# Eight small products and two low parts at other places in one core's adaLN block

## The chip, the cores and the metric

The kernel runs on one core of one Trainium2 chip. The metric is the device time of one execution in microseconds (us). The five engines work through queues of their own and wait for each other by semaphores: TensorE (PE) multiplies matrices into PSUM, VectorE (DVE), ScalarE (ACT) and GpSimd (POOL) do elementwise work, and SyncE (SP) issues most of the transfers.

## The reference

A layer norm with a scale and a shift from a conditioning vector feeds a linear-attention block, and its result is added to x; a second layer norm of the same kind feeds a bilinear GLU without a nonlinearity, which is added again:

```
h = _layernorm(x) * (1 + ca) + sa
x = x + ga * _A_ref(h, A_wqkv, A_wo)          # 2048 x 512, 32 heads of 16
h = _layernorm(x) * (1 + cb) + sb
x = x + gb * _B_ref(h, w_gate, w_up, w_down)  # ((h Wg) * (h Wu)) Wd, F = 1376
```

Everything is float32. This study concerns the second half, from the GLU on.

## The kernel before

Each float32 operand is split into a high part h (rounded by an ACT copy) and a low part l = x - h (a subtraction on DVE or POOL), and each product is three matmuls, h·h, h·l and l·h.

**The blocks.** The 2048 tokens are four chunks of 512, taken in two sides: side 0 is chunks 0 and 1, side 1 chunks 2 and 3. The 1376 columns of the GLU are eleven f tiles, ten of 128 and f tile 10 (`tail`) of 96. The main loop goes over 22 blocks, n = 0 to 21: eleven f tiles of side 0, then eleven of side 1. The text names a block by n: blocks 11 and 12 are the first two of side 1, block 21 is the last (f tile 10 of side 1). A block computes the gate and up products of both chunks with Strassen's seven products (Winograd's form), each of six matmuls of 512 columns, in four PSUM banks a, b, c, d. In order they are: a11 into a, s1 into d, s2 into b, a12 into a, s3 into c, a22 into c, s4 into d. Between them ACT and DVE copy and add banks: c22 = d + u3 (L1113) reads d behind s3; c12 = d + u2 (L1122) reads d behind s4; phi (L1083) are the two elementwise products of gate and up. The s1 of the next block overwrites d.

**The points.** Between the products lie named points, `a11`, `s1`, `s2`, `a12`, `s3`, `pe`, `mid`, `s4`, at each of which a list of small jobs is run, in the list's order. `s3` and `pe` follow each other with no product between them; `mid` lies between a22 and s4; `s4` is the end of the block. The order in which the code runs is the order on every engine's queue.

**The down products.** f tiles are paired, and a pair's product with w_down is again done by seven products, in a form with 256 columns: `pair_steps` returns seven steps (L1226 on PE, with the adds to x, L1253, on DVE). They wait in `queue`, and a block pops one at each of the points s1, s1, a12, a12, pe, pe, s4. The high and low parts of a pair's operands come from `Pair.second` and `Pair.lows` (L1168 on ACT, L1172 on DVE or POOL). f tile 10 has no partner. Its eight products of side 0, one for each chunk and each 128 tokens, are in the list `alone`: a single product is three matmuls of 512 columns with 96 rows (L1146, L1147, L1148), one add to x on DVE (L1153), and the store of x on SP's queue (L1155). Four singles are run in block 11 and four in block 12. All pair steps and singles take a bank from a pool of four PSUM banks, `acc`; a bank is free again when DVE has added it to x.

**Transfers.** The right operands of later blocks (right, seven loads for a block, L1044) and the rows of w_down (raw, L111) are loaded on SP's queue, in the order of the code, behind the stores of x. The raw rows are scaled on DVE (L1280) before they are split.

Of the kernel before, what the change touches and what calls it, by code (L numbers as in the profile page):

```python
# [22 lines left out]
def tile_adaln_block(  # L23
# [24 lines left out]
    NF = len(fts)  # L48
# [1383 lines left out]
    tail = groups[-1][-1]  # L1432
# [8 lines left out]
    for n, (s, g, f) in enumerate(order):  # L1441
# [10 lines left out]
        at = {p: list(early.get((n, p), ())) for p in ("a11", "s1", "s2", "s3", "mid", "s4", "pe")}  # L1452
# [39 lines left out]
        if (s, f) in pair_of:  # L1492
            at_first = f == groups[g][0]
            p = pairs.setdefault((s, g), Pair())
# [20 lines left out]
        if was and was[:2] in paired and was[2] == groups_of[was[0]][was[1]][1]:  # L1515
            of, p = was[0], pairs[was[:2]]
            points = POINTS if queue else POINTS[4:]
            queue += [x for js in ((0, 1), (2, 3))[:1 if (s, f) == (1, tail) else 2] for x in pair_steps(of, p, js)]
            if of:
                at["s2"].append(lambda p=p: (p.lows("s1", "s2"), p.second("s4")))  # L1520
                at.setdefault("a12", []).append(lambda p=p: p.lows("a12", "s4", "a22"))
            else:
                at["s2"].append(lambda p=p: p.second("s1", "s2"))
                at.setdefault("a12", []).append(lambda p=p: p.lows("s1", "s2", "a22", "a12"))
                at["pe"].append(lambda p=p: p.second("s4"))
                at["s4"].append(lambda p=p: p.lows("s4"))
        for x in points if queue else ():
            at.setdefault(x, []).append(lambda: queue and queue.pop(0)())
        points = POINTS
        if s == 1 and alone:  # L1530
            for x in ("s3", "pe", "mid", "s4"):
                at[x].insert(0, lambda: alone.pop(0)())
        if f == tail and s == 1:
            at["s3"].append(lambda: split_down(1, tail))
# [66 lines left out]
```

## Time and profile before

| | us |
|---|---|
| median of 3 runs (lowest, highest) | 556.5 (555.55, 557.04) |
| the profiled execution | 555.82 |
| its span, first to last instruction | 553.4 |
| PE busy in the span | 546.1 |
| DVE busy | 432.5 |
| ACT busy | 299.7 |
| POOL busy | 177.6 |

The profile is of one execution. A row of its timeline has the start from the span's start, the duration, the engine, the line in the kernel, the operation with its output and inputs, and how many such instructions were merged; in brackets stands how long the engine was idle before it, and what ended that. PE rows give the weights' shape and the output's. SPq is SP's sequencer, which issues transfers. The mean granted clock of TensorE over the span is 0.998 of full speed.

### The profile page before, as it was taken

Reading aid. Unit: us, or ns where it says so; the run is one execution under the profiler, and the core shown is the slowest. Engines: PE = TensorE matmul, PEld = TensorE weight load, DVE = VectorE, ACT = ScalarE, POOL = GpSimd, SP = SyncE. Lnnn points to the kernel's source line nnn. Section 1 sums busy time; section 2 is a strip of 40 time slices with the busy share of each in tenths; the row PEclk is TensorE's granted clock in tenths of the full one; section 3 lists DMA queues with packets and bytes.
Section 4 is the critical chain, followed back from the end, with each engine's and each line's share of the span. In section 5 each row is a group of like instructions: output and inputs, shape, how many; then the busy total and the mean of one; then the engine's idle time right before and its main releaser. Section 6 shows DMA issues by size and latency. Waiting matters only on the chain.

```text
span 553.4 us, 8143 instructions
## 1 busy us (share of the span) xinstructions
PE 546.1 (99%) x2775; PEld 460.0 (83%) x2775; DVE 432.5 (78%) x794; ACT 299.7 (54%) x535; POOL 177.6 (32%) x180
## 2 busy tenths in 40 slices
PE   7999999999999999999999999999999999999997
PEld 6888888888888888888888888878888888888886
DVE  5978779978998998865655766896676877779696
ACT  4876858456467876654545355553243535443540
POOL 2000000003527646353556644540003524242400
PEclk9999999999999999999999999999999999999999
DMA  8910224203230045194888634299667534442004
GB/s 248 374 62 1 76 77 152 77 0 78 78 114 2 0 161 181 39 322 173 284 286 279 215 123 172 77 341 390 199 217 259 176 129 139 136 145 78 1 0 153
DMA packets 58512, 83.24 MB, mean 150 GB/s; under 512 B 6564, under 2 KB 23720, under 8 KB 58472
## 3 DMA queue, kind: packets, MB, share of 16 engines
q1 hardware_dynamic: 56544, 81.16, 43.2%
q10 hardware_dynamic: 1928, 1.58, 1.0%
q8 instruction: 22, 0.36, 0.3%
q14 instruction: 18, 0.15, 0.1%
HBM read 53.02 MB, written 29.69 MB: 149 GB/s over the span
## 4 chain that ended last, share of the span: by engine, by line
PE 94%; DVE 3%; DMA 2%; issue 0%; ACT 0%; POOL 0%; DVEq 0%; ACTq 0%; POOLq 0%
PE bank L1057 36%; PE acc L1226 9%; PE acc L871 8%; PE bank L219 5%; PE bank L221 5%; PE bank L220 5%; PE acc L1147 3%; PE acc L1146 3%; PE acc L1148 3%; PE acc L372 3%; PE acc L374 3%; PE acc L373 3%; PE bank L284 2%; PE acc L459 2%; PE bank L846 1%; DMA raw<-in_B_w_down_dram 1%
## 5 line engine op out<-in xcount | busy, mean ns | idle before, releaser
L1057 PE MATMUL bank<-h,w 128*128 128x512 f32 (+1 forms) x924 | 222.2, 391 | 0.2 <-DVE g L1122 0.2
L1057 PEld LDWEIGHTS bank<-h,w 128*128 128x128 f32 (+1 forms) x924 | 168.1, 186 | 36.4 <-DVE g L1122 0.6
L1063 ACT ACTIVATE bank<-bank 128x512 f32<-128x512 f32 (+2 forms) x46 | 26.2, 571 | 123.8 <-PE bank L1057 123.6
L1253 DVE TENSOR_TENSOR x<-acc,x 128x256 f32<-128x256 f32 x132 | 48.0, 415 | 12.9 <-PE acc L1226 12.2
L1226 PE MATMUL acc<-w,kh 128*128 128x256 f32 x308 | 57.4, 283 | 0.4 <-DVE x L1253 0.4
L1226 PEld LDWEIGHTS acc<-w,kh 128*128 128x128 f32 x308 | 50.6, 191 | 4.4 <-DVE x L1253 0.6
L1020 POOL TENSOR_TENSOR w<-raw,w 128x256 fp32r<-128x256 f32 (+3 forms) x22 | 24.7, 1124 | 73.7 <-ACT w L1013 64.1
L219 PE MATMUL bank<-w,h 128*128 128x512 f32 x112 | 44.1, 394 | 0.0
L221 PE MATMUL bank<-w,h 128*128 128x512 f32 x112 | 43.7, 390 | 0.0
L220 PE MATMUL bank<-w,h 128*128 128x512 f32 x112 | 43.7, 390 | 0.0
L1226 PE MATMUL acc<-w,kl 128*128 128x256 f32 x154 | 43.5, 283 | 0.0
L871 PE MATMUL acc<-w,xh 128*128 128x512 f32 x128 | 40.7, 399 | 0.0
L712 POOL TENSOR_TENSOR f<-h,zb 128x512 f32<-128x512 f32 x12 | 17.4, 1470 | 62.9 <-ACT zb L692 48.8
L262 POOL TENSOR_TENSOR rstd<-ve,half 128x4 f32<-128x4 f32 (+3 forms) x12 | 11.2, 936 | 81.6 <-DVE ve L259 68.5
L1063 ACT ACTIVATE u<-bank 128x512 f32<-128x512 f32 (+1 forms) x44 | 26.2, 595 | 15.4 <-PE bank L1057 15.2
L1083 DVE TENSOR_TENSOR phi<-bank,g 128x512 f32<-128x512 f32 (+1 forms) x22 | 15.1, 687 | 24.2 <-PE bank L1057 24.2
L1113 DVE TENSOR_TENSOR g<-bank,u 128x512 f32<-128x512 f32 (+1 forms) x22 | 15.2, 690 | 21.2 <-ACT u L1063 19.9
L1020 POOL TENSOR_TENSOR w<-t,w 128x512 fp32r<-128x512 f32 (+1 forms) x22 | 29.7, 1351 | 0.0
L1153 DVE TENSOR_TENSOR x<-acc,x 128x512 f32<-128x512 f32 x44 | 27.8, 680 | 2.3 <-PE acc L1148 2.3
L1147 PE MATMUL acc<-w,kh 128*128 128x512 f32 (+1 forms) x76 | 29.6, 390 | 0.0
L1146 PE MATMUL acc<-w,kh 128*128 128x512 f32 (+1 forms) x76 | 29.6, 390 | 0.0
L1148 PE MATMUL acc<-w,kl 128*128 128x512 f32 (+1 forms) x76 | 29.6, 389 | 0.0
(204 smaller groups left out, 1184.0 us busy)
## 6 DMA issues: line engine op xcount, KB each, us to landing
right<-w SPq DMA_DIRECT2D x56, 256.0 KB, 3.6
w<-right SPq DMA_DIRECT2D x56, 256.0 KB, 3.7
x<-in_A_x_dram SPq DMA_DIRECT2D x22, 256.0 KB, 5.3
raw<-in_w_mod_dram SPq DMA_DIRECT2D x22, 256.0 KB, 3.7
raw<-in_B_w_down_dram SPq DMA_DIRECT2D x18, 256.0 KB, 2.9
side_s<-h SPq DMA_DIRECT2D x16, 256.0 KB, 2.5
h<-side_s SPq DMA_DIRECT2D x16, 256.0 KB, 5.4
raw<-in_A_wqkv_dram SPq DMA_DIRECT2D x12, 256.0 KB, 5.9
```

Of the source, the lines that this page charges most:

```text
L219: nc.tensor.matmul(ps, ah, bh, start=begin and i == 0, stop=False)
L220: nc.tensor.matmul(ps, ah, bl, start=False, stop=False)
L221: nc.tensor.matmul(ps, al, bh, start=False, stop=end and i == n - 1)
L871: nc.tensor.matmul(yps[i], x, y, start=fresh and k + n == 0, stop=k == KD - 1 and n == 2, skip_group_check=True)
L1020: sub = lambda out, x, y: (on or nc.gpsimd).tensor_tensor(out, x, f32(y), op=ALU.subtract)
L1057: mm = lambda x, y, **kw: nc.tensor.matmul(ps, x[:, k], y, skip_group_check=True, **kw)
L1063: nc.scalar.activation(out, x, AF.Copy)
L1146: nc.tensor.matmul(dn[j], hh[:n, a:b], dh[:n], start=i == 0, stop=False)
L1147: nc.tensor.matmul(dn[j], hh[:n, a:b], dl[:n], start=False, stop=False)
L1148: nc.tensor.matmul(dn[j], hl[:n, a:b], dh[:n], start=False, stop=i == n_of - 1)
L1226: mm = lambda x, y, **kw: nc.tensor.matmul(ps, x[:, a:b], y, skip_group_check=True, **kw)
L1253: nc.vector.tensor_tensor(xt[:, halves[at]], banks[b][m], xt[:, halves[at]], op=ALU.add)
```

## The change

```diff
@@ -1518,7 +1518,8 @@
             if of:
                 at["s2"].append(lambda p=p: (p.lows("s1", "s2"), p.second("s4")))
-                at.setdefault("a12", []).append(lambda p=p: p.lows("a12", "s4", "a22"))
+                if f != tail:
+                    at.setdefault("a12", []).append(lambda p=p: p.lows("a12", "s4", "a22"))
...
@@ -1527,8 +1528,10 @@
         for x in points if queue else ():
             at.setdefault(x, []).append(lambda: queue and queue.pop(0)())
         points = POINTS
+        if (s, f) == (1, tail):
+            at["a12"].append(lambda p=p: p.lows("a12", "s4", "a22"))
         if s == 1 and alone:
-            for x in ("s3", "pe", "mid", "s4"):
+            for x in ("s3", "s3", "pe", "pe") if n == NF else ("s3", "s3", "pe", "pe"):
                 at[x].insert(0, lambda: alone.pop(0)())
```

There are two edits. In blocks 11 and 12 the four singles stood at s3, pe, mid and s4; they now stand two at s3 and two at pe, which is one place on PE, between the products s3 and a22 (both arms of the conditional are the same). In block 21 the low parts of a12, s4 and a22 of the last pair stood ahead of the two pair steps at a12; they now stand behind them.

On PE, block 12: the rows with acc are singles (each three rows), bank_2389 is the product a22 into c, bank_2390 the product s4 into d. This piece of the difference shows the second single's end and the two that move up:

```order
 L1147 MATMUL acc_4526<-w_4317,kh_4289 128x512
 L1148 MATMUL acc_4526<-w_4316,kl_4290 128x512
+L1146 MATMUL acc_4532<-w_4316,kh_4285 128x512
+L1147 MATMUL acc_4532<-w_4317,kh_4285 128x512
+L1148 MATMUL acc_4532<-w_4316,kl_4286 128x512
+L1146 MATMUL acc_4538<-w_4316,kh_4285 128x512
+L1147 MATMUL acc_4538<-w_4317,kh_4285 128x512
+L1148 MATMUL acc_4538<-w_4316,kl_4286 128x512
 L1057 MATMUL bank_2389<-h_4232,w_3849 128x512
 L1057 MATMUL bank_2389<-h_4233,w_3849 128x512
```

The third and fourth single left the places behind a22 and behind s4 and now stand ahead of a22; twelve matmuls of singles follow each other.

On DVE, block 12, before: the adds of the singles are L1153, g_4518 is c22, phi_4551 and phi_4554 the products, g_4550 is c12.

```order
L1113 TENSOR_TENSOR g_4518<-bank_2390,u_4516 128x512
L1153 TENSOR_TENSOR x_99<-acc_4520,x_99 128x512
L1153 TENSOR_TENSOR x_101<-acc_4526,x_101 128x512
L1153 TENSOR_TENSOR x_131<-acc_4538,x_131 128x512
L1083 TENSOR_TENSOR phi_4551<-bank_2389,g_4518 128x512
L1122 TENSOR_TENSOR g_4550<-bank_2390,u_4490 128x512
L1083 TENSOR_TENSOR phi_4554<-g_4492,g_4550 128x512
L1153 TENSOR_TENSOR x_133<-acc_4556,x_133 128x512
```

And the same place now:

```order
L1113 TENSOR_TENSOR g_4518<-bank_2390,u_4516 128x512
L1153 TENSOR_TENSOR x_99<-acc_4520,x_99 128x512
L1153 TENSOR_TENSOR x_101<-acc_4526,x_101 128x512
L1153 TENSOR_TENSOR x_131<-acc_4532,x_131 128x512
L1153 TENSOR_TENSOR x_133<-acc_4538,x_133 128x512
L1083 TENSOR_TENSOR phi_4557<-bank_2389,g_4518 128x512
L1122 TENSOR_TENSOR g_4556<-bank_2390,u_4490 128x512
L1083 TENSOR_TENSOR phi_4560<-g_4492,g_4556 128x512
```

The fourth add moved from behind the block's last phi to the other three. On SP's queue the order is unchanged: four stores of x, seven loads of right, two of w_down.

On DVE, block 21: s_5883 is the sum s4 of the pair, kl are low parts (5845 of a12, 5886 of s4), the rows L1253 the adds of the two pair steps at a12, g_5925 is c22.

```order
 L1182 TENSOR_TENSOR s_5883<-phi_5818,s_5852 128x512
-L1172 TENSOR_TENSOR kl_5845<-phi_5818,kh_5844 128x512
-L1172 TENSOR_TENSOR kl_5886<-s_5883,kh_5885 128x512
 L1253 TENSOR_TENSOR x_1867<-acc_5785,x_1867 128x256
 L1253 TENSOR_TENSOR x_1869<-acc_5785,x_1869 128x256
 L1253 TENSOR_TENSOR x_2045<-acc_5783,x_2045 128x256
 L1253 TENSOR_TENSOR x_2047<-acc_5783,x_2047 128x256
+L1172 TENSOR_TENSOR kl_5845<-phi_5818,kh_5844 128x512
+L1172 TENSOR_TENSOR kl_5886<-s_5883,kh_5885 128x512
 L1113 TENSOR_TENSOR g_5925<-bank_2390,u_5923 96x512
```

The two low parts changed places with the four adds.

## The prediction

> **What bounds the kernel now.** I began with the page: the busy shares, the clock, the chain of waits.
>
> ```profile
> PE 546.1 (99%) x2775; PEld 460.0 (83%) x2775; DVE 432.5 (78%) x794; ACT 299.7 (54%) x535; POOL 177.6 (32%) x180
> PEclk9999999999999999999999999999999999999999
> PE 94%; DVE 3%; DMA 2%; issue 0%; ACT 0%; POOL 0%; DVEq 0%; ACTq 0%; POOLq 0%
> ```
>
> TensorE (PE) is busy almost from end to end at a full clock. The change neither adds nor removes a matmul, so it can only open or close gaps between matmuls. The list of waits on PE, for the whole span, says how much there is to win:
>
> ```profile
> PE acc L153 <- DVE w L148: 2.0, 1, 2.0
> PE bank L295 <- ACT n L277: 1.0, 1, 1.0
> PE acc L1226 <- DVE x L1253: 0.4, 1, 0.4
> PE bank L1057 <- DVE g L1122: 0.2, 1, 0.2
> ```
>
> The first two are in the first 10 us, far from the change. This list counts from the modelled end of a matmul, and modelled ends overlap; a gap is better read from start to start. One of 512 columns starts 0.23 us after its predecessor, one of 256 columns 0.12 us after it, as these pieces of the chain show:
>
> ```profile
> 387.85 1.36 PE bank L1057 x6
> 393.35 1.43 PE acc L1226 x12
> ```
>
> Against these pitches I read the timeline of the stretches that the edits touch. Blocks are counted as in the program's loop: 11 and 12 carry the moved products, 21 is the last. Three gaps stand out. The first is in block 11:
>
> ```profile
> 382.61 0.40 PE L1146 MATMUL acc<-w,kh 96*128 96x512 f32 x1
> 383.44 0.69 DVE L1113 TENSOR_TENSOR g<-bank,u 128x512 f32<-128x512 f32 x1 [1.26 <-ACT u L1063]
> 384.00 0.40 PE L1226 MATMUL acc<-w,kh 128*128 128x256 f32 x2
> 384.05 1.28 DVE L1153 TENSOR_TENSOR x<-acc,x 128x512 f32<-128x512 f32 x2
> 384.60 0.28 PE L1226 MATMUL acc<-w,kl 128*128 128x256 f32 x1
> 384.79 0.51 PE L1226 MATMUL acc<-w,kh 128*128 128x256 f32 x2
> ```
>
> The matmul at 384.79 opens the pair step "d" in a bank that the first single product still holds until VectorE (DVE) has added it to x. That add starts at 384.05 and, being one of two in 1.28 us with 0.68 each, ends at 384.73; PE goes on 0.06 later. It starts 0.19 after its predecessor instead of 0.12, and its pair takes 0.51 instead of 0.40, a restart that costs 0.11. Together 0.18 us.
>
> The second is at the end of block 13:
>
> ```profile
> 402.33 5.27 SPq L1155 DMA_DIRECT2D out_dram<-x  x4
> 407.69 3.25 SPq L1044 DMA_DIRECT2D w<-right  x7
> 411.06 1.05 SPq L111 DMA_DIRECT2D raw<-in_B_w_down_dram  x2
> 414.35 0.74 DVE L1253 TENSOR_TENSOR x<-acc,x 128x256 f32<-128x256 f32 x2
> 416.63 1.29 DVE L1280 TENSOR_TENSOR raw<-raw,row 128x512 f32<-128x512 f32 x2 [1.54 <-DMA raw<-in_B_w_down_dram]
> 417.41 1.55 PE L1057 MATMUL bank<-h,w 128*128 128x512 f32 x6
> 417.84 0.68 DVE L1083 TENSOR_TENSOR phi<-bank,g 128x512 f32<-128x512 f32 x1
> 418.44 0.68 DVE L1122 TENSOR_TENSOR g<-bank,u 128x512 f32<-128x512 f32 x1
> 419.18 1.67 PE L1057 MATMUL bank<-h,w 128*128 128x512 f32 x6 [0.22 <-DVE g L1122]
> ```
>
> DVE stands 1.54 us at the scaling of the w_down rows, which land late; phi and c12 (L1122) queue behind it, and PE needs c12 read before it overwrites bank d. PE was due at 417.41 + 1.36 = 418.77 and starts at 419.18: 0.41, with 1.67 - 1.55 = 0.12 for the restart, 0.5 us in all.
>
> The third is in block 21:
>
> ```profile
> 528.55 0.68 DVE L1182 TENSOR_TENSOR s<-phi,s 128x512 f32<-128x512 f32 x1
> 529.15 0.68 DVE L1172 TENSOR_TENSOR kl<-phi,kh 128x512 fp32r<-128x512 f32 x1
> 530.06 0.69 DVE L1172 TENSOR_TENSOR kl<-s,kh 128x512 fp32r<-128x512 f32 x1 [0.23 <-ACT kh L1168]
> 530.67 1.41 DVE L1253 TENSOR_TENSOR x<-acc,x 128x256 f32<-128x256 f32 x4
> 530.83 0.28 PE L1226 MATMUL acc<-w,kl 128*128 128x256 f32 x1
> 531.47 0.51 PE L1226 MATMUL acc<-w,kh 128*128 128x256 f32 x2 [0.37 <-DVE x L1253]
> 532.00 0.68 DVE L1113 TENSOR_TENSOR g<-bank,u 96x512 f32<-96x512 f32 x1
> 532.30 2.95 PE L1057 MATMUL bank<-h,w 128*96 128x512 f32 x12
> ```
>
> The next "d" step again lacks a bank: the adds that free it (L1253) stand behind two low parts (L1172), the second of which waits for ScalarE. PE is due 0.12 after 530.83, at 530.95, and starts at 531.47: 0.52, and 0.11 for the restart, 0.63 us.
>
> **The change part by part.** Low parts of the last block. DVE's order becomes s, four adds, two low parts. The adds start at 529.15 and take 1.41, and the pair that frees the bank (half of them) is through before 530. PE's "d" at 530.95 no longer waits: -0.63. What is late next? The low parts end at 530.56 + 2 x 0.6 = 531.8 and c22 (L1113) behind them at 532.4, instead of 532.7 before, since it too lay behind the waiting low part. PE overwrites d in the second half of the twelve matmuls from 532.30, half of 2.95 later and now 0.63 earlier, at 533.1: spare 0.7. The low parts themselves are read by pair steps behind those twelve matmuls, past 534. POOL's low part of a22 has no other place in POOL's order. Nothing here costs.
>
> Singles in block 11. All twelve matmuls now run from 382.61 at (384.00 - 382.61) / 6 = 0.232 each, to 385.39; "a" follows, and "d" 0.72 later at 386.11. DVE's four adds start at 384.05 and end at 384.73, 385.33, 385.93 and 386.53 (0.60 from one to the next). Four banks are in turn: "a" takes the first single's (free 384.8, needed 385.4), its ScalarE seed the second's, "d" the third's, free at 385.93 + 0.06 = 385.99, needed at 386.11. The gap closes with 0.12 to spare: -0.18. From both sides: were the third bank a whole add late, the gap would be 0.6 - 0.12 + 0.11 = 0.6; nothing excludes a few hundredths of wait. I take no wait, since every term is a row of this place.
>
> The Trainium skill speaks against this: VectorE: DVE Perf Modes, The DRAIN you can't avoid, says that an operation does not start until the pipe of the one before is empty. By that rule the adds would stand 0.68 apart, the third would end at 386.1, and with the restart 0.15 us of the gap would stay, which would make the sum below 1.16. The two adds of this trace, 1.28 us for both, do not bear it out.
>
> Singles in block 12. This block has no pair steps behind its singles, so what they covered matters more:
>
> ```profile
> 400.19 0.40 PE L1146 MATMUL acc<-w,kh 96*128 96x512 f32 x1
> 401.62 1.28 DVE L1153 TENSOR_TENSOR x<-acc,x 128x512 f32<-128x512 f32 x2
> 403.66 1.53 PE L1057 MATMUL bank<-h,w 128*128 128x512 f32 x6
> 405.22 0.69 DVE L1122 TENSOR_TENSOR g<-bank,u 128x512 f32<-128x512 f32 x1
> 405.72 6.97 PE L1057 MATMUL bank<-h,w 128*128 128x512 f32 x30
> 406.55 0.68 DVE L1153 TENSOR_TENSOR x<-acc,x 128x512 f32<-128x512 f32 x1
> ```
>
> The fourth single used to lie between the last product into d and the next block. That cover goes. Now: singles from 400.19 to 402.97, two products of 1.36 to 405.69, the next block's first 1.36, and d is overwritten at 407.05. The last product into d starts at 404.33; c12 starts 405.22 - 403.66 = 1.56 behind that, at 405.89, and is done at 406.58. Spare 0.4 us, so no cost; were phi or an add in front of it, 0.68 more would cost PE 0.3 and the restart. The adds no longer stand there: they run from 401.62 at 0.60 and are done at 404.1.
>
> Its queue. The four stores of x keep their places on SP's queue, and behind them the seven loads of right parts and the two of w_down. The last store waited for the add that ended at 407.23; the loads began at 407.69, 0.46 later. With the add done at 404.1 they begin at 404.56, and w_down is issued 411.06 - 407.69 = 3.37 after that, at 407.9 instead of 411.06.
>
> ```profile
> raw<-in_B_w_down_dram SPq DMA_DIRECT2D x2, 256.0 KB, 5.6
> DMA  0980000079977268878999999999999999999999
> ```
>
> This is the DMA view of 405 to 420 us: 5.6 us to landing, and idle engines in front of the first loads. So it lands near 414, and DVE comes to it at 414.35 + 0.74 = 415.1: no wait, scaling done by 416.4, phi by 417. The last product into d starts at 413.95 + 1.36 = 415.31 and c12, 1.56 behind it, is done at 417.6, more than a microsecond before 418.77. Gap closed: -0.5. Bounds: nothing won if the landing does not move, and 1 us lost for each that it moves back.
>
> **Sum.** 0.18 + 0.5 + 0.63 = 1.31. The profiled execution spans 553.4 and took 555.82 with the 2.4 around it; it becomes 552.1 and 554.5. The median of the three runs, 556.5, lies 0.7 above it. Laid on the median the sum gives 555.2, on the mean of all four executions (556.23) 554.9; I take 555.0. A measurement of this kernel tells about 0.3%, 1.67 us, from no change, so the bound for faster is 554.83, and the forecast stands just on its near side.
>
> **Rivals.** First, w_down does not land earlier. For it: four stores and seven loads of 256 KB now go out closer together in front of it, on the same queue. Against: the idle slices above. Only 0.81 is won: 555.7 on the median.
>
> Second, the run of four singles makes a wait of its own in block 11, the third bank an add late. For it: 0.12 is a thin margin. Against: nothing else stands on DVE there. 0.6 in place of 0.18: the sum falls to 0.7, 555.8 on the median.
>
> Third, and slower: w_down lands later, because the packed stores slow the loads in front of it. It decides from a landing of 416.6 on, where DVE now stands still and each microsecond goes straight to c12 and PE. The other gaps give 0.81, so the kernel is slower from 417.4, and by over 0.3% from 419.1; at 420 it would be 3.4 - 0.81 = 2.6 slower, 559.1. Against it: that is 12 us after the issue, where 5.6 were seen.
>
> That the change does nothing is out: it moves instructions at all three gaps.
>
> **How the numbers follow.** Forecast 0.64, first rival 0.12, second 0.12, third 0.12. The three runs lie 1.49 us apart, so a forecast 0.2 us from the bound falls on either side nearly evenly: 0.35 faster, 0.29 same. The first two rivals leave 0.06 for faster and 0.18 for same, the third is slower. Faster 0.41, same 0.47, slower 0.12. Low end 554.0: runs lie up to 0.95 under their median. High end 557.0: the gains lost and runs at their highest; most of the third rival is left out.
>
> **What would show it.** In the changed profile: no PE wait on DVE near 386, 419 or 531; a span near 552.1; w_down issued near 408 and no DVE wait for it in block 13; DVE's four L1153 adds in one piece of some 2.5 us in blocks 11 and 12. The prediction is wrong if PE waits for c12 at the start of block 13, if the "d" step in block 11 starts late, or if a new wait for a DMA shows on DVE or ScalarE.

## The result and the profile after

| | before | after |
|---|---|---|
| median of six executions each (us) | 556.6 (555.55 to 557.04) | 554.12 (553.13 to 554.53) |
| ratio, 95% interval | | 0.9953 (0.994 to 0.9966) |
| the profiled execution | 555.82 | 554.12 |
| its span | 553.4 | 552.4 |
| what lies around the span | 2.4 | 1.7 |

The kernel is faster by 0.47%, 2.5 us on the medians. The forecast was 555.0, a hair short of what it took for a change that can be measured; the time lies 0.9 below it, inside the range. The last two rows of the table already hold the surprise: only 1.0 of the 1.7 us between the two profiled executions is in the span, and 0.7 lies outside it. In the medians below, executions with a granted clock under 0.998 are left out; the ratios and their intervals hold all executions.

The first page of the profile after, its busy times:

```profile
PE 545.8 (99%) x2775; PEld 460.1 (83%) x2775; DVE 432.2 (78%) x794; ACT 299.5 (54%) x535; POOL 176.8 (32%) x180
PEclk9999999999999999999999999999999999999999
```

The same work at the same clock. The list of what PE waited for, after:

```profile
PE acc L153 <- DVE w L148: 2.0, 1, 2.0
PE bank L295 <- ACT n L277: 0.6, 1, 0.6
PE bank L1057 <- POOL w L1020: 0.2, 1, 0.2
```

Both rows in which PE waited for DVE behind the start of the kernel (L1253 and L1122) are gone. A new row, 0.2 on POOL's L1020, stands near 361 us, ahead of both edits. To see what the main loop gained, the same matmuls are compared in the two traces: the last of the first pair step behind 368 us, and the last matmul of the kernel. Before:

```profile
368.42 0.28 PE L1226 MATMUL acc<-w,kl 128*128 128x256 f32 x1
549.41 0.28 PE L1547 MATMUL bank<-w,kl 96*128 96x256 f32 x1
```

After (L1550 is the old L1547, three lines further down):

```profile
361.48 6.74 PE L1057 MATMUL bank<-h,w 128*96 128x512 f32 x28 [0.16 <-POOL w L1020]
368.64 0.28 PE L1226 MATMUL acc<-w,kl 128*128 128x256 f32 x1
548.23 0.28 PE L1550 MATMUL bank<-w,kl 96*128 96x256 f32 x1
```

At 368 us the changed kernel is 0.22 behind, in code that is the same; at the end it is 1.18 ahead. From the first edit to the last it gained 1.40, where the prediction's three gaps made 1.31. The 0.22 and a tail that is 0.18 longer (552.4 - 548.23 against 553.4 - 549.41) leave 1.0 of it in this pair of spans.

Block 11 in the timeline after:

```profile
384.25 2.47 DVE L1153 TENSOR_TENSOR x<-acc,x 128x512 f32<-128x512 f32 x4
385.56 0.40 PE L1226 MATMUL acc<-w,kh 128*128 128x256 f32 x2
385.92 0.40 PE L1226 MATMUL acc<-w,kh 128*128 128x256 f32 x2
386.28 0.41 PE L1226 MATMUL acc<-w,kh 128*128 128x256 f32 x2
```

The four adds are one piece of 2.47. With 0.68 for the last they start (2.47 - 0.68) / 3 = 0.60 apart, the third ends near 384.25 + 2 x 0.60 + 0.68 = 386.13, and "d" starts at 386.28, two steps of 0.36 behind "a" and with a pair of 0.41, so without a restart. Before, it started 0.79 behind "a" and its pair took 0.51.

The way to block 13, from SP's queue and the engines' timeline after:

```profile
402.35 2.12 SPq L1155 DMA_DIRECT2D out_dram<-x  x4
404.57 4.19 SPq L1044 DMA_DIRECT2D w<-right  x7
409.30 0.81 SPq L111 DMA_DIRECT2D raw<-in_B_w_down_dram  x2
405.90 0.69 DVE L1122 TENSOR_TENSOR g<-bank,u 128x512 f32<-128x512 f32 x1 [0.67 <-PE bank L1057]
415.04 1.28 DVE L1280 TENSOR_TENSOR raw<-raw,row 128x512 f32<-128x512 f32 x2
416.88 0.69 DVE L1122 TENSOR_TENSOR g<-bank,u 128x512 f32<-128x512 f32 x1
417.39 2.91 PE L1057 MATMUL bank<-h,w 128*128 128x512 f32 x12
```

The loads start at 404.57 and w_down goes out at 409.30, 1.76 earlier than before. DVE's scaling (L1280) no longer waits for it, c12 (L1122) is done at 417.57, and the first two products of block 14, of which the second overwrites d, are one run of twelve matmuls.

Block 21 after:

```profile
528.60 1.40 DVE L1253 TENSOR_TENSOR x<-acc,x 128x256 f32<-128x256 f32 x4
529.93 0.67 DVE L1172 TENSOR_TENSOR kl<-phi,kh 128x512 fp32r<-128x512 f32 x1
530.39 0.40 PE L1226 MATMUL acc<-w,kh 128*128 128x256 f32 x2
530.53 0.68 DVE L1172 TENSOR_TENSOR kl<-s,kh 128x512 fp32r<-128x512 f32 x1
530.75 0.40 PE L1226 MATMUL acc<-w,kh 128*128 128x256 f32 x2
531.13 0.68 DVE L1113 TENSOR_TENSOR g<-bank,u 96x512 f32<-96x512 f32 x1
```

The adds run first, the pair steps keep their pitch of 0.36, and the second low part meets no wait.

### The profile page after: what moved, and what is told of

It is laid out like the page before. It is cut to its first block, busy times and chain, and to the rows that moved or that the text cites. A ratio compares the mean times of both kernels' runs of the same rounds, so it can differ in the third digit from the quotient of the medians.

```text
span 552.4 us, 8146 instructions
## 1 busy us (share of the span) xinstructions
PE 545.8 (99%) x2775; PEld 460.1 (83%) x2775; DVE 432.2 (78%) x794; ACT 299.5 (54%) x535; POOL 176.8 (32%) x180
## 5 line engine op out<-in xcount | busy, mean ns | idle before, releaser
L1253 DVE TENSOR_TENSOR x<-acc,x 128x256 f32<-128x256 f32 x132 | 48.0, 414 | 13.7 <-PE acc L1226 13.1
L1020 POOL TENSOR_TENSOR w<-raw,w 128x256 fp32r<-128x256 f32 (+3 forms) x22 | 24.7, 1121 | 73.7 <-ACT w L1013 64.1
L1020 POOL TENSOR_TENSOR w<-t,w 128x512 fp32r<-128x512 f32 (+1 forms) x22 | 29.6, 1346 | 0.0
L277 ACT ACTIVATE n<-x,nmr,rstd 128x512 f32<-128x512 f32 x31 | 23.6, 808 | 10.9 <-DVE nmr L267 10.7
```

Of the source, the lines that this page charges most:

```text
L1020: sub = lambda out, x, y: (on or nc.gpsimd).tensor_tensor(out, x, f32(y), op=ALU.subtract)
L1253: nc.vector.tensor_tensor(xt[:, halves[at]], banks[b][m], xt[:, halves[at]], op=ALU.add)
```

## The experiments

All were timed in five rounds beside the kernel before. The first row is the 29 executions of before beside the next four runs; the 27 and the 23 beside the others lie close to them (medians 556.22 and 556.14, spans 554.05 and 554.0, 2.3 outside in both). "Outside" is device time less span, the median over executions. The three columns on the right count the instructions of each engine in the program as built, waits included, which the profile's counts leave out.

| run | ratio (95%) | time | span | outside | DVE | ACT | POOL |
|---|---|---|---|---|---|---|---|
| before | | 556.38 | 554.0 | 2.35 | 956 | 670 | 318 |
| same_before | 1.0005 (0.9994 to 1.0016) | 556.36 | 554.2 | 2.34 | 956 | 670 | 318 |
| both_again | 0.9959 (0.9947 to 0.9971) | 554.25 | 552.4 | 1.76 | 960 | 668 | 319 |
| singles_moved | 0.9983 (0.997 to 0.9996) | 554.83 | 553.1 | 1.73 | 960 | 668 | 319 |
| lows_moved | 1.0014 (0.9994 to 1.0033) | 556.22 | 553.8 | 2.41 | 956 | 670 | 318 |
| singles_11 | 0.9996 (0.9988 to 1.0005) | 556.25 | 554.2 | 2.11 | 960 | 669 | 317 |
| singles_12 | 0.9977 (0.9967 to 0.9986) | 555.40 | 553.4 | 1.99 | 957 | 669 | 319 |
| sums_late | 0.9981 (0.9968 to 0.9994) | 555.48 | 553.5 | 2.00 | 957 | 669 | 318 |
| pad_dve4 | 0.9999 (0.9991 to 1.0008) | 556.56 | 554.6 | 1.96 | 960 | 670 | 318 |
| pad_act2 | 0.9951 (0.9938 to 0.9965) | 553.78 | 552.1 | 1.73 | 960 | 670 | 319 |
| pad_both | 0.9999 (0.9984 to 1.0014) | 556.34 | 554.5 | 1.77 | 960 | 670 | 319 |
| pad_more | 0.9964 (0.9952 to 0.9976) | 554.41 | 552.5 | 1.99 | 968 | 668 | 321 |
| split_later | 0.9967 (0.9955 to 0.9979) | 554.48 | 552.8 | 1.73 | 960 | 668 | 319 |

**Both kernels again**, unedited.

> The kernel before, unchanged, timed against itself. Theory 1 (the gain is the three closed gaps on PE, 1.4 us by the two traces, and the rest of the measured 2.48 us is how the executions of before happened to lie): ratio 1.000 within 0.001, and over several executions the span and the time outside it scatter by a microsecond (553.4 and 2.4 in the one profile so far). Theory 2 (the change also saves about 0.7 us outside the span, 2.42 us before against 1.72 after): every execution of this kernel has about 2.4 us outside its span.

> The changed kernel again, beside the three others. Theory 1: 1.4 us faster than before, ratio 0.9975, the sum of the two halves; a repeat of 0.9953 would mean that the gaps are not all of it. Theory 2: 2.1 to 2.5 us faster, ratio 0.9955 to 0.9962, with about 1.7 us outside the span.

Both repeat. Against 29 executions of before the changed kernel gains 2.1 us: 1.6 in the span, 0.6 outside it.

**The two halves.** The first edit alone:

```diff
-            for x in ("s3", "pe", "mid", "s4"):
+            for x in ("s3", "s3", "pe", "pe") if n == NF else ("s3", "s3", "pe", "pe"):
                 at[x].insert(0, lambda: alone.pop(0)())
```

> The first edit alone: singles two at s3 and two at pe in blocks 11 and 12, low parts of block 21 where they were. Theory 1: the gaps in blocks 11 and 13 close (0.2 and 0.5 us), the one of 0.65 in block 21 stays; 0.7 us faster than before, ratio 0.9987. Theory 2: the saving outside the span comes with the stores that go out earlier, so 1.4 us or more faster, ratio 0.9975 or less, with 1.7 us outside the span.

The span falls by 0.9, and the whole 0.6 outside comes with this edit. The second alone:

```diff
-                at.setdefault("a12", []).append(lambda p=p: p.lows("a12", "s4", "a22"))
+                if f != tail:
+                    at.setdefault("a12", []).append(lambda p=p: p.lows("a12", "s4", "a22"))
...
+        if (s, f) == (1, tail):
+            at["a12"].append(lambda p=p: p.lows("a12", "s4", "a22"))
```

> The second edit alone: low parts of block 21 behind its two pair steps, singles where they were. Theory 1: the gap in block 21 closes, 0.65 us faster, ratio 0.9988; the gaps in blocks 11 and 13 stay as before. Theory 2: if the end of the program gains outside the span by finishing its stores in another order, 1.3 us or more faster, ratio 0.9977 or less.

Only 0.2 is gained in the span, where 0.63 was forecast, and nothing outside. Its timeline shows why one cannot read the edit from its median alone:

```profile
416.52 1.29 DVE L1280 TENSOR_TENSOR raw<-raw,row 128x512 f32<-128x512 f32 x2 [1.82 <-DMA raw<-in_B_w_down_dram]
417.02 1.55 PE L1057 MATMUL bank<-h,w 128*128 128x512 f32 x6
419.07 1.66 PE L1057 MATMUL bank<-h,w 128*128 128x512 f32 x6 [0.50 <-DVE g L1122]
...
530.82 0.41 PE L1226 MATMUL acc<-w,kh 128*128 128x256 f32 x2
531.19 0.40 PE L1226 MATMUL acc<-w,kh 128*128 128x256 f32 x2
```

The gap in block 21 is closed (pairs 0.37 apart), but at the end of block 13, which this kernel does not touch, PE was due at 417.02 + 1.36 = 418.38 and starts at 419.07: 0.69, against 0.41 in the execution on which the forecast was built. There 0.28 went back.

**One block at a time.** The singles moved in block 11 alone, and in block 12 alone:

```diff
-            for x in ("s3", "pe", "mid", "s4"):
+            for x in ("s3", "s3", "pe", "pe") if n == NF else ("s3", "pe", "mid", "s4"):
```

> The singles moved in block 11 alone; blocks 12 and 21 as before. In the span: only the gap near 385 us closes, 0.2 us; the gap of 0.5 at the end of block 13 stays, because the stores of block 12 leave as late as before. Outside the span: this kernel has 960 instructions on DVE, 669 on ScalarE and 317 on POOL; theory A gives 1.75 us, a theory of POOL's count (318 before, 319 in the changed kernel) 2.35. By A 0.8 us faster in all, ratio 0.9986.

```diff
-            for x in ("s3", "pe", "mid", "s4"):
+            for x in ("s3", "pe", "mid", "s4") if n == NF else ("s3", "s3", "pe", "pe"):
```

> The singles moved in block 12 alone; blocks 11 and 21 as before. In the span: the gap near 385 stays, the one near 419 closes, 0.5 us, with w_down issued near 409. Outside: 957 instructions on DVE, 669 on ScalarE, 319 on POOL; theory A gives about 2.35 us if a single instruction more is not enough, a theory of POOL's count 1.75. By A 0.5 us faster in all, ratio 0.9991.

The timeline of the kernel with block 11 alone:

```profile
385.87 0.40 PE L1226 MATMUL acc<-w,kh 128*128 128x256 f32 x2
386.59 0.41 PE L1226 MATMUL acc<-w,kh 128*128 128x256 f32 x2
417.56 1.36 DVE L1280 TENSOR_TENSOR raw<-raw,row 128x512 f32<-128x512 f32 x2 [2.08 <-DMA raw<-in_B_w_down_dram]
417.75 1.55 PE L1057 MATMUL bank<-h,w 128*128 128x512 f32 x6
420.16 1.20 PE L1057 MATMUL bank<-h,w 128*128 128x512 f32 x4 [0.87 <-DVE g L1122]
```

And with block 12 alone:

```profile
384.00 0.28 PE L1226 MATMUL acc<-w,kl 128*128 128x256 f32 x1
384.19 0.50 PE L1226 MATMUL acc<-w,kh 128*128 128x256 f32 x2
414.38 1.28 DVE L1280 TENSOR_TENSOR raw<-raw,row 128x512 f32<-128x512 f32 x2
416.78 2.91 PE L1057 MATMUL bank<-h,w 128*128 128x512 f32 x12
```

Each closes its own gap and leaves the other: "d" 0.72 behind "a" in the first, 0.19 behind its predecessor with a restart (0.50) in the second; PE waiting for c12 in the first, twelve matmuls in one run in the second. Block 12 carries the gain, 0.6 in the span. Block 11's 0.18 is too small to be seen in a median, and in this execution the unmoved gap of 420.16 - (417.75 + 1.36) = 1.05 at the end of block 13 covers it.

**Is it the late rows, or what queues behind them?** The kernel before, with the scaling of w_down and its sums put behind the last phi of block 13, the singles where they were:

```diff
                     if s:
-                        at["mid"].insert(0, sums)
+                        at["s4" if n == 13 else "mid"].insert(0, sums)
```

> The kernel before with one thing changed: in block 13 the scaling of the w_down rows and the weight sums stand at s4 instead of mid, so on DVE they stand behind phi and c12. Singles and low parts are where they were. If late w_down rows cost PE their time only because c12 stands behind the scaling on DVE: the gap near 419 us closes although the rows land as late as before (near 416.6), 0.5 to 0.7 us off the span, about 0.09 off the time outside (957 instructions on DVE), ratio 0.9989. If something else delays PE there, the gap stays.

Its timeline:

```profile
416.76 0.69 DVE L1122 TENSOR_TENSOR g<-bank,u 128x512 f32<-128x512 f32 x1 [0.67 <-PE bank L1057]
417.27 2.91 PE L1057 MATMUL bank<-h,w 128*128 128x512 f32 x12
418.09 1.28 DVE L1280 TENSOR_TENSOR raw<-raw,row 128x512 f32<-128x512 f32 x2
```

c12 now waits for PE alone, and PE does not stop. No store and no load moved. So the late rows cost time only through c12 in the queue behind them; the span falls by 0.5, about as with block 12's singles.

**The time outside the span.** The first edit brings, besides its moves, four more instructions on DVE and one on POOL, two fewer on ACT; DVE's and POOL's are waits that the other order of buffers needs. Two explanations: the stores that end earlier, or the bare number of instructions. Four tiny writes on DVE, at the start of the kernel before, into a tile that nothing reads:

```diff
+    pad = consts.tile([P, 4], F32, name="pad")
+    for i in range(4):
+        nc.vector.memset(pad[:, i:i + 1], 0.0)
```

> The kernel before with four tiny memsets more on DVE near the start, where it is idle; DVE then has 960 instructions, as in the changed kernel, instead of 956. Theory A (the 0.6 us outside the span comes from the number of instructions on DVE, since the instructions that are loaded behind the last one of the program come earlier): 1.75 us outside the span instead of 2.35, the span as before (554.0), ratio 0.999. Theory B (it comes from the earlier stores of x or from another engine's count): 2.35 us outside, ratio 1.000.

And two on ACT in the changed kernel, which takes away its difference there:

```diff
+    pad = consts.tile([P, 2], F32, name="pad")
+    for i in range(2):
+        nc.scalar.activation(pad[:, i:i + 1], eps_phi, AF.Copy)
```

> The changed kernel with two tiny activations more on ScalarE near the start; ScalarE then has 670 instructions as in the kernel before, instead of 668. Theory A: nothing changes, 1.75 us outside the span, ratio to the kernel before 0.996. Theory C (ScalarE's two instructions fewer are the cause): 2.35 us outside, ratio 0.997.

ACT has no part in it (1.73 as without). Four on DVE give 0.4 of the 0.6. singles_11 also has four more on DVE, but one fewer on POOL, and lies at 2.11; its expectation had 1.75 by DVE's count or 2.35 by POOL's, and neither came. singles_12, with one more on each, lies at 1.99, again between its 1.75 and 2.35. Then four on DVE and one on POOL in the kernel before:

```diff
+    pad_p = consts.tile([P, 1], F32, name="pad_p")
+    for i in range(1):
+        nc.gpsimd.memset(pad_p[:, i:i + 1], 0.0)
...
+    pad = consts.tile([P, 4], F32, name="pad")
+    for i in range(4):
+        nc.vector.memset(pad[:, i:i + 1], 0.0)
```

> The kernel before with four tiny memsets more on DVE and one on POOL near the start: 960 and 319 instructions, as in the changed kernel. Theory A, as the last runs left it (each instruction more on DVE takes about 0.09 us off the time outside the span, each on POOL about 0.2, ScalarE's count does nothing): 1.75 us outside the span instead of 2.33, the span unchanged near 554.1, ratio 0.999. If the time outside belonged to the moved stores, it stays at 2.0 or above.

This gives 1.77 (1.73 to 1.84 over its executions, against 1.9 to 2.5 of before), the whole fall, with every store and product where it was. Last, eight on DVE and two on POOL in the changed kernel, the same edit with other numbers:

> The changed kernel with eight tiny memsets more on DVE and two on POOL near the start: 968 and 321 instructions. Theory A: the time outside the span falls further, below 1.5 us, down to a floor that no run has shown yet, and the kernel is up to 1 us faster than the changed one, ratio to before 0.994. If the effect was a single boundary that is passed, it stays at 1.75 us, ratio 0.996, and if the next boundary costs again it goes back up to 2.3.

It rose to 1.99 instead of falling further. A rule by which each instruction takes off its share is wrong. The two pads on before bring no time at the medians: the time outside is 0.4 and 0.6 shorter, but their spans are 554.6 and 554.5 against 554.0. The spans of before scatter from 553.1 to 555.3, so it is not shown whether a pad lengthens the span or these executions lay high. The two profiled executions of before and pad_both have the same span, 553.4, and took 555.82 and 555.18. A part of the scatter is at the end of block 13. What PE waited for there in kernels that keep before's order at that place, first same_before:

```profile
PE bank L1057 <- DVE g L1122: 0.2, 1, 0.2
```

then pad_dve4 and pad_both (their added lines shift the numbers):

```profile
PE bank L1060 <- DVE g L1125: 0.6, 1, 0.6
```

```profile
PE bank L1063 <- DVE g L1128: 0.9, 1, 0.9
```

One gap, in the same order of work, is 0.2 to 0.9 wide by this list (0.50 with the low parts alone, above), as the rows of w_down happen to land.

**One more gap.** Near 539 us a pair step waits 0.07 for a bank. In the changed kernel, the split of f tile 10's products behind the first two closing pair steps:

```diff
-    flush()
...
     while queue:
         queue.pop(0)()
         more.pop(0)()
+        flush()
```

> The changed kernel with one thing more: behind block 21 the split of f tile 10's products comes after the first two pair steps of the closing part instead of ahead of them. The last gap of the changed kernel in this half, near 539 us, is of the same kind as those that closed (adds that free a bank stand behind other DVE work): it closes, 0.17 us off the span, the time outside unchanged at 1.75, ratio to before 0.9955. If PE then waits for the split parts instead, the time is the same or up to 0.5 us longer.

A miss: the adds that free the bank now stand behind low parts that wait for ACT, as its DVE and PE rows show:

```profile
537.09 1.29 DVE L207 TENSOR_TENSOR kl<-phi,kh 96x512 fp32r<-96x512 f32 x2 [0.61 <-ACT kh L206]
538.30 0.74 DVE L1253 TENSOR_TENSOR x<-acc,x 128x256 f32<-128x256 f32 x2
539.10 0.50 PE L1226 MATMUL acc<-w,kh 128*128 128x256 f32 x2 [0.43 <-DVE x L1253]
```

The gap grew and the span is 0.4 longer than both_again's. None of the variants beats the changed kernel; pad_act2 is its equal within the intervals.

## Why the prediction was right and where it failed

**The gaps.** All three closed, by the mechanism named for each, and the main loop of the profiled execution gained 1.40 for 1.31. singles_11, singles_12 and lows_moved show that each edit closes its own.

**Block 11.** The bank that was to be free 0.12 ahead of need was so by 386.28 - 386.13 - 0.06 = 0.09, with the 0.06 of the prediction. The rule of the Trainium skill that was weighed there (VectorE: DVE Perf Modes, The DRAIN you can't avoid) does not hold for these adds: four of 0.68 start 0.60 apart. That section of the Trainium skill itself names an exception, which the prediction passed over: an operation that is not held starts earlier. The trace agrees with the exception.

**Block 12 and SP's queue.** c12 was forecast at 405.89 and started at 405.90; the loads were forecast at 404.56 and started at 404.57. The issue of w_down was forecast at 407.9 and came at 409.30. The 3.37 from the first load to w_down was carried over from before; it became 4.73. The loads were not slower to issue: the first six went out in 2.81. SP then waited for stores of x to land, once ahead of the seventh load and once ahead of w_down, as its waits from 404.4 to 409.5 us show:

```profile
SPq L1044 <- DMA out_dram<-x: 1.0, 1, 1.0
SPq L111 <- DMA out_dram<-x: 0.5, 1, 0.5
```

In the kernel before, whose four stores went out over 5.27 instead of 2.12, these rows have no wait for a store; both_again, singles_12 and pad_more have it as the changed kernel does (1.0, 1.1 and 1.2 ahead of a load). So the stores in front did hold w_down back, near to what the first rival said, but this ate only part of the spare: the rows had landed by 415.04, when DVE came to them, against 415.1 in the forecast. The gap at the end of block 13 was costed at 0.5, and at the medians singles_12 and sums_late put it at 0.6 and 0.5.

**Block 21.** The order and the spare were as forecast. -0.63 by the rows of before, and no wait left.

**The sum.** Here the prediction failed, in its words "took 555.82 with the 2.4 around it; it becomes 552.1 and 554.5": the 2.4 was carried over as a constant, and no reason was given for it. It is 1.73 after, and those 0.6 us are what lies between a forecast on the near side of 0.3% and a result beyond it. pad_both shows that no moved work is needed for it, only four more instructions on DVE and one on POOL. What they change is open. One trail is in the transfers around the end. The DMA view of 551 to 557 us (forty slices of 0.15 us) for the kernel before:

```profile
GB/s 287 362 321 171 89 48 0 0 0 0 0 0 0 0 0 0 0 0 55 0 0 0 0 0 0 0 0 0 0 0 55 0 0 0 0 0 0 0 0 0
q14 instruction: 2, 0.02, 0.9%
```

the same for pad_both:

```profile
GB/s 191 48 294 348 226 7 0 0 0 0 0 0 0 0 0 0 0 0 55 0 0 0 0 55 0 0 0 0 0 0 0 0 0 0 0 0 0 0 0 0
```

Behind the span's end at 553.4 there are two transfers of the instruction queue, the second 12 slices (1.8 us) behind the first in before, 5 slices (0.75 us) in pad_both. But the distance of the two does not settle the time outside. In singles_11 (553 to 559 us, span 555.1) it is only 4 slices (0.6 us), with 2.15 outside in that execution:

```profile
GB/s 48 21 27 7 0 0 0 0 0 0 0 0 0 0 0 0 0 55 0 0 0 55 0 0 0 0 0 0 0 0 0 0 0 0 0 0 0 0 0 0
```

and pad_more (551 to 557 us, span 552.7) has a single transfer there, with 1.71 outside:

```profile
GB/s 21 0 0 0 0 0 0 0 0 0 0 0 0 55 0 0 0 0 0 0 0 0 0 0 0 0 0 0 0 0 0 0 0 0 0 0 0 0 0 0
```

What the device waits for at its end stays open, and so does why that depends on the instructions; pad_more fits no simple count, and sums_late, with one more instruction on DVE than before, lies at 2.00, where a quarter of pad_dve4's fall would make it 2.25.

**What the sum leaves.** The spans' medians fell by 1.6, not 1.31. The halves alone gave 0.9 and 0.2, 1.1 together. With spans of one kernel that scatter over 2 us (553.1 to 555.3 in before's 29) and a gap that is 0.4 wide in one execution and 1.05 in another of an order that is the same there, the remaining 0.3 is not settled. The forecast took the gap from one execution. From start to start, the gap at the end of block 13 is 0.41, 0.39, 0.69, 1.05, 0.81 and 1.14 in the profiled executions of before, same_before, lows_moved, singles_11, pad_dve4 and pad_both, which keep before's order there. Their mean is 0.75, 0.34 more than the forecast's 0.41, and of the size of what is missing; but singles_12 and sums_late, which close this gap, show no more than 0.6 and 0.5 at the medians.

## What to carry to other kernels

Keep the span and the time around it apart, in the forecast and in the result: here an edit that only reorders changed the number of waits, and the time outside the span fell with it by as much as the largest gap that was closed. On an engine that works in order, put what frees a bank ahead of work that nobody waits for yet, and look for what is queued behind an instruction that waits for a transfer: moving that instruction back can be worth as much as an earlier transfer. A gap that hangs on a landing is sized from several executions, not from one. And when stores move up in a queue, look for what waits behind them until they have landed.

## What the runs showed of the hardware

The device time around the span took 1.73 to 2.41 us at the medians of these kernels, and was 1.77 instead of 2.35 with five tiny writes at the start of the program, though the device time itself did not fall at the medians. On SP's queue, four stores of 256 KB that went out within 2.12 us made a later load wait 1.0 to 1.2 us until a store had landed; over 5.27 us they made none wait. And PE paid 0.10 on top of a short wait: in singles_12 the pair that came 0.07 late (384.19) took 0.50, and in split_later the pair behind a wait of 0.43 (539.10) took 0.50 as well, where the other pairs take 0.40.
